# Hash attention and max-out FFN: the projection's split moved to GpSimd, and the last part of w_out loaded earlier, into output tiles

## The chip, the cores and the metric

The kernel runs on one core of one Trainium2 chip. The metric is the device time of a run in microseconds (us), less is better. Engines are called PE (TensorE, matrix multiply), DVE (VectorE), ACT (ScalarE), POOL (GpSimd) and SP (SyncE, which issues most of the DMAs).

## The reference

Attention in which a query sees only the keys that fall in the same hash bucket, followed by a feed-forward layer with a maximum of three products. Batch 4, 8 heads, 768 positions, head size 64, 6 hash bits, model width 512, feed-forward width 768.

```python
q_bits = (einsum('bhsd,dk->bhsk', q, proj) > 0)          # 6 bits of each query
k_bits = (einsum('bhsd,dk->bhsk', k, proj) > 0)
mask   = bucket(q_bits)[..., :, None] == bucket(k_bits)[..., None, :]
scores = where(mask, q @ k.T / sqrt(64), -1e9)
attn   = softmax(scores) @ v                             # (4, 8, 768, 64)
x      = attn.transpose(0, 2, 1, 3).reshape(3072, 512)
h      = maximum(maximum(x @ w1, x @ w2), x @ w3)        # (3072, 768)
out    = h @ w_out                                       # (3072, 512)
```

## The kernel before

The work is cut by batch `b` (0 to 3), pair of heads `pr` (0 to 3) and half of the positions `hf` (0 or 1). For each pair, q, k and v are loaded in float32 (0.39 MB each). q and k are split into two halves in float16 (`split_h`, L266 or L268, and `split_r`, L273), side by side in a tile `s`. That tile is transposed into `T`, in batch 0 and in the first two pairs of batch 1 by PE (L292), later by a DMA transpose on SP's queue (`xbar`, L282). `hash_mm` (L310 and L312) multiplies `T` by `PAB`, the projection in two float16 parts. DVE turns the results into bits, PE transposes these, and they go by way of DRAM (`bit_out`, L349, called the bounce's write, `bit_in`, L352, its read, `T<-dr`) into six rows of `T`. A score matmul (`score`, L395) then gives score and hash agreement at once; ACT takes exponentials (`expo`, L401), and `attend` (L413) multiplies by v. v is cast to float16 by POOL in batch 0 and by ACT (L202) later, where POOL adds it up (`vsum`, L363 to L366) for a small matmul (`svp`, L376). DVE normalizes into `xn`.

For each half of the positions, `xn` becomes `xT` (by PE for the first half, then by a DMA transpose, `x_bar`, L457). `l1` (L478, into `ps`) multiplies by w1, w2 and w3, in 6 blocks of features `fb`, and DVE takes the maximum into `ht` (L487; the first of three is copied, L202 on ACT or L204 on DVE). `l2` (L496, into `po`) multiplies the six `ht` by the six row chunks of `wout_sb`; the result is copied to an output staging tile `osb` (five of them) and stored (L507).

The order of instructions on every engine is fixed when the program is built, by a planner: each task has an engine or two to choose from, an estimated duration, a priority, the tasks it needs, and the counted buffers it takes and gives. The planner runs a small simulation and emits each task at its turn. So the planner's guesses set the order, and the chip keeps to it. Memory on PE's output side is in banks: two for scores (`sc`), one for `av`, three (`mm`) for everything else.

`make_p` makes `PAB` from `p32`, the projection as loaded by ACT's queue at the start: a cast to float16 (`ph`, L234), a difference (`pr32`, L235), and four scalings into `PAB` (L238). It is one task, planned for DVE.

The weights come in parts. w1 and w2 and half of w3 are loaded by POOL's queue with a cast on the way. The second half of w3 (two parts) and w_out (three parts of two row chunks each, 128 x 2 x 512 float32, 0.52 MB) are loaded by SP's queue in float32 into `ws`, of which there are two, by `stage_w`, and cast by POOL into place by `cast_w`:

```python
parts.append(add(("POOL", 1.5 if w == "o" else 1.1), -60, [ld], lambda e, w=w, i=i: cast_w(w, i, e),
                 give=("ws",)))
```

Part 0 has chunks 0 and 1, part 1 has 2 and 3, part 2 has 4 and 5. On SP's queue parts 0 and 1 stand behind the bounce of pair (1,1). Then come q, k and v of pair (2,0), the DMA transpose of pair (1,3), part 2 of w_out, the transpose to `xT` of batch 0's second half, the bounce's write of pair (1,2), and the transpose of pair (2,0). A part takes one of the two `ws`, so part 2 can be loaded only when POOL has cast part 0.

Of the kernel before, what the change touches and what calls it, by code (L numbers as in the profile page):

```python
# [8 lines left out]
FP32 = mybir.dt.float32  # L9
FP16 = mybir.dt.float16  # L10
AluOp = mybir.AluOpType
# [122 lines left out]
def kernel(  # L134
# [12 lines left out]
    nc = tc.nc  # L147
    B, H, S, D = q.shape
    NBITS = proj.shape[1]
    P = 128  # L150
    NCH = S // P
    DM = H * D
# [34 lines left out]
    op = ctx.enter_context(tc.tile_pool(name="op", bufs=OSB))  # L187
# [12 lines left out]
    def copy(e, o, i):  # L200
        if e == "ACT":
            nc.scalar.copy(o, i)  # L202
        else:
            ENG[e].tensor_copy(o, i)  # L204

    p32 = konst.tile([D, NBITS], FP32, name="p32")
# [16 lines left out]
    PAB = konst.tile([P, 2 * NBITS], FP16, name="PAB")  # L223
    xn0 = konst.tile([P, 2, NP, CH, P], FP16, name="xn0")
    w_sb = [konst.tile([P, NJ, DF], FP16, name=f"w{i}_sb") for i in range(3)]
    wout_sb = konst.tile([P, NF, DM], FP16, name="wout_sb")
# [4 lines left out]
    def make_p(e):  # L231
        ph = konst.tile([D, NBITS], FP16, name="ph")
        pr32 = konst.tile([D, NBITS], FP32, name="pr32")
        nc.vector.tensor_copy(ph[:], p32[:])  # L234
        nc.vector.tensor_tensor(out=pr32[:], in0=p32[:], in1=ph[:], op=AluOp.subtract)  # L235
        for o in (0, D):
            for i, src in enumerate((ph, pr32)):
                nc.vector.tensor_scalar(out=PAB[o : o + D, NBITS * i : NBITS * (i + 1)], in0=src[:],  # L238
                                        scalar1=1024.0, scalar2=None, op0=AluOp.mult)


# [1 line left out]
    src = {"q": q, "k": k, "v": v}  # L243
# [279 lines left out]
    def both(dve, act):  # L523
        return [("DVE", dve), ("ACT", act)]

    tp = add("DVE", -200, [], make_p) if False else None
    loads, ready_T, ready_v, ready_m, wload = {}, {}, {}, {}, {}

# [3 lines left out]
    for i, (n, pr, heads) in enumerate(order):  # L532
        half = heads != (0, 2)
        loads[n, 0, pr, heads] = add(("SP", 0.45), -400 + i, [], lambda e, n=n, pr=pr, heads=heads: load(n, 0, pr, heads, e),
                                     take=(n,) if heads[0] == 0 else (), xfer=0.55 if half else 1.1)
    mp = add(("DVE", 0.5), -300, [add(("ACT", 0.1), -500, [], lambda e: None, lat=3.2)], make_p)

    def load_w(i, half, e):
# [111 lines left out]
    wst_tiles = {}  # L650

    def w_view(w, i):
        c = slice(2 * i, 2 * i + 2)
        if w == "o":
            return moe_w_out.rearrange("(c p) m -> p c m", p=P)[:, c, :], wout_sb[:, c, :]
        f = slice(w[0] * DF // 2, (w[0] + 1) * DF // 2)
        return (moe_w1, moe_w2, moe_w3)[w[1]].rearrange("(c p) f -> p c f", p=P)[:, c, f], w_sb[w[1]][:, c, f]

    def stage_w(w, i, e):
        from_dram = w_view(w, i)[0]  # L660
        t = wst.tile([P, 2 * DM], FP32, tag="ws", name="ws")
        wst_tiles[w, i] = t[:, 0 : 2 * from_dram.shape[2]].rearrange("p (c f) -> p c f", c=2)
        nc.sync.dma_start(wst_tiles[w, i], from_dram)  # L663

    def cast_w(w, i, e):
        copy(e, w_view(w, i)[1], wst_tiles.pop((w, i)))

    def weights(b, pr, parts):
        if (pr or b) and parts[0] not in plain and parts[0] != "o":
            prev = add(("POOL", 0.1), -150, [bounced[b, pr]], lambda e: hold(b, pr, e), after=[wprev[0]])  # L670
        elif pr or b:
            prev = bounced[b, pr]
        else:
            prev = ready_v[0, 0]
        for w in parts:
            if w == "o" or w in plain:
                parts = []
                for i in range(NF // 2) if w == "o" else range(NJ // 2):
                    ld = add(("SP", 0.5), -60 if w == "o" else -70, [], lambda e, w=w, i=i: stage_w(w, i, e), take=("ws",),
                             xfer=1.4 if w == "o" else 1.1, after=[prev])  # L680
                    prev = ld
                    parts.append(add(("POOL", 1.5 if w == "o" else 1.1), -60, [ld], lambda e, w=w, i=i: cast_w(w, i, e),
                                     give=("ws",)))
                wload[w] = plan.join(parts, ())
                continue
            else:
                prev = add(("POOL", 0.8), -100, [], lambda e, w=w: load_w(w[1], w[0], e), xfer=2.15, after=[prev])
            wload[w] = prev
        wprev[0] = prev
# [116 lines left out]
```

The softmax here doesn't subtract the row's maximum and nothing guards it: scores larger than these inputs give would overflow.

## Time and profile before

| What | Value |
|---|---|
| Median of 5 runs | 268.95 us (266.16 to 269.76) |
| The profiled execution | 268.95 us, span 267.2 us |
| PE busy | 256.6 us (96% of the span) |
| ACT busy | 196.5 us (74%) |
| DVE busy | 176.4 us (66%) |
| POOL busy | 41.8 us (16%) |
| DMA moved | 41.69 MB, mean 156 GB/s |
| Granted PE clock | 1.000 |
| six operations of `make_p` on DVE | 0.16 to 0.17 us each, from 4.30 us |
| third part of w_out | issued at 70.88 us, POOL casts it from 75.54 us |

The span is the time from the first to the last instruction of the profiled execution; what the run took beyond it lies around the program. Times within the execution are counted from the span's start. In a line of the timeline stand start, duration, engine, line, operation, tiles and, in brackets, how long the engine had been idle and what ended that. A name such as SPq is the engine's queue, in which DMAs are issued. The busy share of an engine is a mean over stages in which different things hold the work up.

### The profile page before, as it was taken

How to read it: one execution, taken by the hardware profiler on the slowest of the kernel's cores; microseconds unless marked ns; L12 is line 12 of the kernel's file. 1: busy time of each engine (PE TensorE's matmuls, PEld its weight loads, DVE VectorE, ACT ScalarE, POOL GpSimd, SP SyncE). 2: the span in 40 equal slices, each digit the busy share in tenths (PEclk: the TensorE clock that was granted, in tenths of full speed). 3: DMA queues.
4: the chain of work that ended last, by engine and by line, in shares of the span. 5: the costliest groups of instructions: out<-in, count | busy, mean ns of one | idle time of the engine just before them, and what ended most of it. 6: DMA issues, size and time to landing. Idle time of an engine off the chain costs nothing.

```text
span 267.2 us, 7323 instructions
## 1 busy us (share of the span) xinstructions
PE 256.6 (96%) x2992; PEld 174.2 (65%) x2992; DVE 176.4 (66%) x394; ACT 196.5 (74%) x283; POOL 41.8 (16%) x57
## 2 busy tenths in 40 slices
PE   7997979999989999999999999999999999999995
PEld 7886757766646666677666767765666656555552
DVE  4998669989855899559885796551655535345260
ACT  5897998987925889999889889898899642332422
POOL 1530054183310333003302030000000000000000
PEclk9999999999999999999999999999999999999999
DMA  6994489699998598995996997212130050120303
GB/s 207 367 264 70 131 261 267 180 262 271 235 240 282 179 230 221 212 256 156 209 229 175 234 179 121 51 32 79 42 61 0 4 163 15 42 79 0 120 0 119
DMA packets 67408, 41.69 MB, mean 156 GB/s; under 512 B 48046, under 2 KB 63662, under 8 KB 67374
## 3 DMA queue, kind: packets, MB, share of 16 engines
q1 hardware_dynamic: 64654, 39.26, 57.1%
q0 software_dynamic: 2640, 1.97, 4.8%
q8 instruction: 23, 0.38, 0.6%
q14 instruction: 11, 0.09, 0.1%
q10 hardware_dynamic: 80, 0.00, 0.0%
HBM read 25.72 MB, written 6.84 MB: 122 GB/s over the span
## 4 chain that ended last, share of the span: by engine, by line
PE 72%; DMA 15%; DVE 5%; SPq 2%; POOL 2%; issue 1%; ACT 0%; ACTq 0%; POOLq 0%
PE ps L478 30%; PE sc L395 17%; PE po L496 11%; PE av L413 9%; DMA dr<-bt 5%; DMA q<-in_q_dram 3%; DMA v<-in_v_dram 3%; PE hps L312 2%; DMA ws<-in_moe_w_dram 2%; DMA ws<-in_moe_w_out_dram 2%; DVE s L273 2%; DVE s L268 1%; SPq L250 1%; SPq L663 1%; DVE T L204 1%
## 5 line engine op out<-in xcount | busy, mean ns | idle before, releaser
L401 ACT ACTIVATE AT<-sc 128x768 f16<-128x768 f32 x192 | 146.3, 814 | 16.2 <-PE sc L395 14.2
L478 PE MATMUL ps<-xT,w_sb 128*128 128x384 f16 x576 | 106.3, 326 | 0.3 <-DVE ht L487 0.3
L395 PE MATMUL sc<-T 128*128 128x384 f16 x384 | 93.0, 325 | 2.2 <-DMA T<-dr 1.4
L487 DVE TENSOR_TENSOR ht<-ht,ps 128x384 f16<-128x384 f16 x96 | 52.9, 551 | 46.4 <-PE ps L478 44.0
L413 PEld LDWEIGHTS <-AT 128*128 128x128 f16 x1152 | 59.5, 97 | 22.8 <-issue 0.2
L478 PEld LDWEIGHTS <-w_sb 128*128 128x128 f16 x576 | 52.7, 98 | 30.8 <-issue 0.9
L413 PE MATMUL av<-vone,AT 128*128 128x65 f16 x1152 | 65.5, 193 | 0.0
L395 PEld LDWEIGHTS <-T 128*128 128x128 f16 x384 | 30.2, 97 | 12.8 <-DMA T<-dr 1.5
L496 PE MATMUL po<-wout_sb,ht 128*128 128x512 f16 (+1 forms) x150 | 33.8, 370 | 0.9 <-POOL wout_sb L204 0.9
L202 ACT CAST ht<-ps 128x384 f16<-128x384 f32 x28 | 13.4, 480 | 26.5 <-DVE ht L487 19.1
L202 ACT COPY osb<-po 128x512 f32<-128x512 f32 (+1 forms) x24 | 13.6, 568 | 18.8 <-PE po L496 18.7
L496 PEld LDWEIGHTS <-ht 128*128 128x128 f16 x150 | 14.1, 98 | 14.8 <-DVE rr L436 1.2
L363 POOL TENSOR_TENSOR vt<-v 128x384 f32<-128x384 f32 x12 | 12.6, 1047 | 67.4 <-DMA v<-in_v_dram 67.4
L430 DVE TENSOR_TENSOR t<-av,mv 128x390 f32<-128x390 f32 x32 | 17.9, 560 | 7.4 <-PE av L413 7.3
L449 DVE TENSOR_TENSOR xn<-t,rr 128x384 f16<-128x384 f32 x32 | 20.5, 641 | 1.1
L273 DVE SCALAR_TENSOR_TENSOR s<-q,s 128x384 f16<-128x384 f32 x32 | 19.2, 615 | 3.0 <-ACT s L266 2.9
L273 DVE SCALAR_TENSOR_TENSOR s<-k,s 128x384 f16<-128x384 f32 x32 | 19.6, 632 | 0.2
L204 DVE CAST ht<-ps 128x384 f16<-128x384 f32 x20 | 11.1, 555 | 10.3 <-PE ps L478 10.1
L292 PE MATMUL tps<-iden,s 128*128 128x128 f16 x168 | 13.4, 220 | 0.8 <-DVE bit L322 0.5
L312 PE MATMUL hps<-PAB,T 128*128 128x12 f16 x336 | 10.7, 168 | 1.4 <-DVE T L204 1.4
L292 PEld LDWEIGHTS <-s 128*128 128x128 f16 x168 | 10.6, 99 | 2.1 <-DVE s L273 1.1
L312 PEld LDWEIGHTS <-T 128*128 128x128 f16 x336 | 10.1, 96 | 2.5 <-DVE T L204 1.5
(54 smaller groups left out, 142.3 us busy)
## 6 DMA issues: line engine op xcount, KB each, us to landing
v<-in_v_dram SPq DMA_DIRECT2D x16, 384.0 KB
out_dram<-osb SPq DMA_DIRECT2D x23, 256.0 KB
q<-in_q_dram SPq DMA_DIRECT2D x15, 384.0 KB
k<-in_k_dram SPq DMA_DIRECT2D x15, 384.0 KB
w_sb<-in_moe_w_dram POOLq DMA_DIRECT2D x5, 384.0 KB, 10.4
ws<-in_moe_w_out_dram SPq DMA_DIRECT2D x3, 512.0 KB
ws<-in_moe_w_dram SPq DMA_DIRECT2D x2, 384.0 KB
dr<-bt SPq DMA_DIRECT2D x15, 36.0 KB
```

Source lines behind the costliest of these rows:

```text
L202: nc.scalar.copy(o, i)
L273: nc.vector.scalar_tensor_tensor(out=s[:, a0:a1, D : 2 * D], in0=raw_view(n, b, pr, heads), scalar=QS, in1=s[:, a0:a1, 0:D], op0=AluOp.mul ...
L292: nc.tensor.transpose(p16[:, c * P : (c + 1) * P], S16[b, pr][:, a0 + c, :], iden[:])
L312: nc.tensor.matmul(o, T[b, pr][:, a, :], PAB[:], start=True, stop=True)
L395: nc.tensor.matmul(sc[:, i, 0:HQ], t[:, NA2 + hh * NCH + 2 * j + i, :], t[:, hh * NCH + hf * CH : hh * NCH + (hf + 1) * CH, :], start=True ...
L401: nc.scalar.activation(AT[:], scs.pop(u)[:, :, 0:HQ], ActFn.Exp, bias=EXP_BIAS, scale=EXP_SCALE)
L413: nc.tensor.matmul(av[:, o : o + D + 1], AT[:, i, c * P : (c + 1) * P], vones[b % 2][:, 2 * pr + hh, 2 * j + i, 0 : D + 1], start=slot == ...
L430: nc.vector.tensor_tensor(out=t[:, :, :, 0 : D + 1], in0=av[:, :, :, 0 : D + 1], in1=mv, op=AluOp.add)
L449: nc.vector.tensor_tensor(out=xv, in0=t[:, :, :, 0:D], in1=rr[:].to_broadcast([P, 2, CH, D]), op=AluOp.mult)
L478: nc.tensor.matmul(ps[:, 0:HQ], w_sb[i][:, jc, fb * P : (fb + 1) * P], xTs[b, hf][:, jc, :], start=jc == 0, stop=jc == NJ - 1)
L487: nc.vector.tensor_tensor(out=ht[:], in0=ht[:], in1=ps[:, 0:HQ], op=AluOp.max)
L496: nc.tensor.matmul(ps[:, m0:m1], hts[b, hf, fb][:, c * P : (c + 1) * P], wout_sb[:, fb, m0:m1], start=fb == 0, stop=fb == NF - 1)
```

## The change

First, all six operations of `make_p` are issued on POOL instead of DVE. The planner still counts them as DVE's.

Second, part 2 of w_out is no longer a load of its own. When part 1 is staged, chunks 4 and 5 are loaded ahead of it as two DMAs of 128 x 512 float32 (0.26 MB each) into two `osb` tiles, and when part 1 is cast, POOL casts these two ahead of it. The tasks of part 2 stay in the plan and emit nothing. So the plan, and with it the order of everything else on every engine, stays as it was. On SP's queue the data of part 2 now stand between parts 0 and 1, ahead of q, k and v of pair (2,0) and the transpose of pair (1,3), and nothing stands between that transpose and the one to `xT`. On POOL all casts of w_out stand ahead of the sums of v of pair (2,0). The planner's counts of `ws` and `osb` do not know of the change.

```diff
     def make_p(e):
...
-        nc.vector.tensor_copy(ph[:], p32[:])
-        nc.vector.tensor_tensor(out=pr32[:], in0=p32[:], in1=ph[:], op=AluOp.subtract)
+        nc.gpsimd.tensor_copy(ph[:], p32[:])
+        nc.gpsimd.tensor_tensor(out=pr32[:], in0=p32[:], in1=ph[:], op=AluOp.subtract)
         for o in (0, D):
             for i, src in enumerate((ph, pr32)):
-                nc.vector.tensor_scalar(out=PAB[o : o + D, NBITS * i : NBITS * (i + 1)], in0=src[:],
+                nc.gpsimd.tensor_scalar(out=PAB[o : o + D, NBITS * i : NBITS * (i + 1)], in0=src[:],
                                         scalar1=1024.0, scalar2=None, op0=AluOp.mult)
...
     def stage_w(w, i, e):
+        if w == "o" and i == 2:
+            return
+        if w == "o" and i == 1:
+            for c in (4, 5):
+                wst_tiles[w, c] = op.tile([P, DM], FP32, tag="osb", name="osb")
+                nc.sync.dma_start(wst_tiles[w, c][:], moe_w_out[c * P : (c + 1) * P, :])
         from_dram = w_view(w, i)[0]
...
     def cast_w(w, i, e):
+        if w == "o" and i == 2:
+            return
+        if w == "o" and i == 1:
+            for c in (4, 5):
+                copy(e, wout_sb[:, c, :], wst_tiles.pop((w, c))[:])
         copy(e, w_view(w, i)[1], wst_tiles.pop((w, i)))
```

## The prediction

> **What bounds the kernel now.** I read the page's first two parts, then the waits of TensorE (PE), then the chain of work that ended last, then the timelines of SP, POOL, ACT and DVE around the one place where the two meet.
>
> ```profile
> PE 256.6 (96%) x2992; PEld 174.2 (65%) x2992; DVE 176.4 (66%) x394; ACT 196.5 (74%) x283; POOL 41.8 (16%) x57
> DMA  6994489699998598995996997212130050120303
> ```
>
> PE is busy 96% of 267.2 us and the clock row is 9 throughout. The order of instructions on each engine is fixed, so the time is PE's work plus the places where PE waits; a PE delay in the middle is not given back, since from 90 to 215 us the table by stretches shows PE busy in all but 0.3 us. DMA is saturated from 53 to 80 us (its row, slices of 6.7 us). In the waits of PE between 60 and 90 us one line counts:
>
> ```profile
> PE po L496 <- POOL wout_sb L204: 0.9, 1, 0.9
> ```
>
> The chain of waits between 60 and 86 us (start, duration, what) says how this wait comes about:
>
> ```profile
> 62.99 7.06 DMA v<-in_v_dram
> 70.13 0.75 POOL vt L363
> 70.88 4.61 DMA ws<-in_moe_w_out_dram
> 75.54 1.05 POOL wout_sb L204
> 76.62 0.59 PE po L496 x2
> ```
>
> The third part of w_out is issued at 70.88, lands at about 75.5, is cast by POOL until 76.6, and only then the last two of six matmuls of the first output group run. Why it is issued so late is in SP's queue (start, time in the queue, line, what):
>
> ```profile
> 59.60 2.32 SPq L663 DMA_DIRECT2D ws<-in_moe_w_out_dram  x2
> 61.97 0.47 SPq L250 DMA_DIRECT2D q<-in_q_dram  x1
> 62.49 0.46 SPq L250 DMA_DIRECT2D k<-in_k_dram  x1
> 62.99 0.47 SPq L250 DMA_DIRECT2D v<-in_v_dram  x1
> 63.56 7.21 SPq L282 DMA_TRANSPOSE T<-s  x1
> 70.88 0.52 SPq L663 DMA_DIRECT2D ws<-in_moe_w_out_dram  x1
> 71.49 2.46 SPq L457 DMA_TRANSPOSE xT<-xn  x1
> ```
>
> It stands behind the transpose of pair (1,3), which is itself held up by the 1.15 MB of q, k and v of pair (2,0) ahead of it.
>
> **Edit 1, six small operations from DVE to POOL.** DVE loses six operations of about 0.16 us; from 4.30 to 5.14 us that is 0.84 us of its queue, and the split of k behind them starts up to 0.75 us sooner. What it gains is swallowed here:
>
> ```profile
> 7.95 0.56 DVE L273 SCALAR_TENSOR_TENSOR s<-q,s 128x384 f16<-128x384 f32 x1 [0.39 <-ACT s L266]
> L647 POOL COPY hold<-T x1: 183/183/183, 35.8 to 35.8; 6x1 f16<-6x1 f16 x1
> ```
>
> The chain at the start is q's load (until 7.05), ACT's split (7.07, 0.84 us), then this DVE operation at 7.95. Neither end of it moves; DVE's idle before it grows from 0.39 to about 1.1 us. The hash bits (L322, 8.43) are queued behind it on DVE, so nothing later moves either. Gain 0; without that load as cover it would be worth up to 0.75.
>
> On POOL the six wait for the load of proj. It had landed by 4.30 (DVE ran its cast there without waiting). The nearest POOL row is the copy of 6x1 above, 0.183 us: 6 x 0.18 = 1.1, done by 5.4. The dear end is the 128x128 add of L365, 0.64 us: 6 x 0.64 = 3.8, done by 8.1. The hash matmuls (L310, 7.03 to 7.77) need the result, and the bits read them at 8.43, so they may slip 0.66 us, to 7.69. The edit costs between 0 and 8.1 - 7.69 = 0.4; I take 0. The next POOL work is the cast of v at 9.51, later than both.
>
> **Edit 2, what it takes away.** The third part no longer needs one of the two ws tiles nor the place behind the transpose. The four po matmuls issued from 74.68 take 0.216 us each (six take 1.30 in the chain), so the fifth would have been issued at 75.54; it came at 76.62. At most 1.08 us of PE go (0.9 of pure waiting, the rest is refilling the pipe). What PE would meet next is the hash matmul of pair (1,3), whose transpose was in before the w_out part that landed at 75.5, and then L478 at 80.36, needing xT; neither waited.
>
> **Edit 2, what it moves.** Now 0.52 MB more stands ahead of q, k and v of pair (2,0), as two DMAs of 0.26 MB. This is what I think decides. The cost per part is read from when POOL's casts could start:
>
> ```profile
> 63.80 1.04 POOL L204 CAST wout_sb<-ws 128x1024 f16<-128x1024 f32 x1 [4.39 <-DMA ws<-in_moe_w_out_dram]
> 65.17 1.04 POOL L204 CAST wout_sb<-ws 128x1024 f16<-128x1024 f32 x1 [0.33 <-DMA ws<-in_moe_w_out_dram]
> ```
>
> Two parts of 0.52 MB landed 1.37 us apart. That is the cheap end. The dear end: from 65.17 to v's landing at about 70.1, 1.18 MB took 4.9 us, so 0.52 MB at that rate takes 2.2. A rule of the Trainium skill speaks against the edit more strongly: "DMA: Bandwidth & Descriptors", section "Anatomy of one DMA — SWDGE (gpsimd) path", gives a DMA 2.0 us fixed plus its bytes at 436 GB/s (fitted for DMAs issued by GpSimd). By it two of 0.26 MB are 2 x 2.6 = 5.2 us if they follow one another, and the sum would be +4.1. The row shows 1.37 us for twice the bytes of one of them, so queued loads hide the fixed part. I go by the row, with a little for the second DMA: 1.5 us later for q, k and v.
>
> Who waits for these three:
>
> ```profile
> 68.98 0.56 DVE L268 TENSOR_SCALAR s<-k 128x768 f16<-128x768 f32 x1 [0.43 <-DMA k<-in_k_dram]
> 68.55 1.51 ACT L401 ACTIVATE AT<-sc 128x768 f16<-128x768 f32 x2
> 70.13 0.83 ACT L202 CAST vone<-v 128x768 f16<-128x768 f32 x1
> 70.87 1.50 ACT L401 ACTIVATE AT<-sc 128x768 f16<-128x768 f32 x2
> ```
>
> ACT came to the cast of v at 70.06 and began at 70.13, as v landed: no slack at all. Behind it on ACT are the exponentials of the last four score tiles of this stretch and one ht evacuation. With two sc banks, the score matmuls at 71.94 and 72.45 wait for the exponentials ahead of them, and the attend matmuls up to 74.50 for the rest; PE has nothing else in its order. So PE reaches po about 1.5 us later, at 76.2. DVE already waited 0.43 for k, and will wait some 1.5 more in all, with two ht evacuations (69.93, 71.49) behind it; with three mm banks that stays inside PE's 1.5 us. POOL's sums of v end at about 74.3, before the svp matmul (73.80 + 1.5).
>
> **Edit 2, the rest.** SP issues one DMA more ahead of q (about 0.45 us); the data ahead arrive later than that, so it is hidden. Three POOL casts (0.5, 0.5, 1.04 us, halves of the row) stand ahead of POOL's sums of v, done by about 68, before v is in. Two of the five osb tiles are in use until then; the first output copy is at 77.25. The transpose of (1,3) ends 1.5 us later, but the w_out load behind it is gone: xT, the bounce of (1,2) and the next transpose have the same bytes ahead as before. One change from plain loads to a transpose and back goes too, and around such a change the DMA rate is low (68 GB/s from 69 to 70 us against 263 to 367 from 64 to 67). So I expect nothing late after 77 us.
>
> **Sum.** PE +1.5 (v late) - 1.08 (w_out no longer late) = +0.4; edit 1 adds 0. The profiled execution took 268.95 us (span 267.2 and 1.75 around it), and the median of the five runs is the same 268.95: **269.4 us**. The runs spread from 266.16 to 269.76, so about 1% (2.7 us) is what a measurement of this kernel can tell from no change.
>
> **Rivals.**
> *The load is nearly hidden (0.26).* For it: DMA is not full when w_out starts (115 GB/s from 60 to 61, 199 from 62 to 63), and k's late landing may not recur. If v comes only 0 to 0.7 us later, PE gains 0.4 to 1.08: 267.9 to 268.6. Against it: the queue is served in order and ACT has no slack.
> *The bounce of pair (1,2) comes too late (0.15).* It is the read T<-dr that SP issued at 79.28, behind the transpose of (2,0), which waits for DVE's split of k. The score matmul at 84.91 needs it and ACT stands empty before that. The read took 2.4 us alone (chain, 23.93); 79.28 + 2.4 = 81.7 leaves at most 3.2 us, less in the crowd. If the transfers ahead slip by over 3 us (the rule's 5.2 for the added loads would do it), PE has lost 2 by v already (3 - 1.08) and waits another 0.5 to 2.5 here: 271.5 to 273.5, slower. For it: the queue is full. Against it: the bytes ahead are unchanged.
> *POOL's projection is slow (0.05).* If an operation costs L363's 1.05 us, PAB is ready at 10.6, 2.9 us after 7.69; with +0.4 that is 272.2. The 6x1 copy speaks against it.
> That the third part is not early at all is excluded by SP's order.
>
> **How the numbers follow.** The main case has 0.54 (v 1.4 to 2.2 us late, 269.2 to 270.1). Nearly hidden 0.26, late bounce 0.15, slow POOL 0.05. The range takes in the bounds of v's delay, the hidden case and the spread of the runs: 267.0 to 271.7. Over 1% slower are the late bounce and part of slow POOL, 0.17; over 1% faster needs more than the 1.08 us that PE can gain, so only an unseen gain or spread, 0.08; the rest, 0.75, is within 1%.
>
> **What would show it.** After: no wait of po on wout_sb; ACT idle 1.4 to 2.2 us before the cast of v at about 71.6, put down to the DMA of v; DVE idle longer before L268 of q and k; PE idle in 70 to 76 in place of 76; the first output copy at 77.5 to 78 instead of 77.25; DVE idle about 1.1 us before 7.95. Wrong if v lands as before, if PE waits for T<-dr near 85, or if the first hash matmul waits for POOL.

## The result, and the profile after

The changed kernel's median is 269.63 us over 43 runs (266.76 to 272.62), beside 268.23 us over 80 runs of the kernel before on the same chips (265.68 to 272.04). The ratio is **1.0035, with a 95% interval of 1.0017 to 1.0053**: 0.9 us more (0.5 to 1.4; 0.0035 x 268.23). The ratio leaves out slow runs, among them seven of the changed kernel at 270.8 to 272.6 us, which the medians contain. The forecast was 269.4 us, with 267.0 to 271.7 as its range and "within 1%" as its likeliest case. So the total came out as forecast. Its terms did not: what the forecast adds up around 70 us comes to about nothing, and the place where every profile with the added DMA shows a loss is the end of the program, which it left out. That is what the rest is about. Microseconds for a ratio are always worked out on 268.2 us.

The profiled execution of the changed kernel took 268.62 us (span 266.8), less than its median and less than the 268.95 of before. One profile of each can't show a difference of 0.9 us; it can show where waits went. First, the rows of PE and DMA on the page of the changed kernel:

```profile
PE 256.8 (96%) x2992; PEld 175.1 (66%) x2992; DVE 174.5 (65%) x388; ACT 196.8 (74%) x283; POOL 44.6 (17%) x64
DMA  6994599699998897998992995302030060110303
```

PE's work is unchanged. DVE has lost six instructions, POOL has gained seven (six of `make_p`, and two casts of half a part for one of a whole). SP's queue in the changed kernel (start, time in the queue, line, what) is as the diff says:

```profile
59.27 0.92 SPq L665 DMA_DIRECT2D osb<-in_moe_w_out_dram  x2
60.29 1.62 SPq L669 DMA_DIRECT2D ws<-in_moe_w_out_dram  x1
61.95 0.48 SPq L250 DMA_DIRECT2D q<-in_q_dram  x1
62.48 0.47 SPq L250 DMA_DIRECT2D k<-in_k_dram  x1
62.99 0.47 SPq L250 DMA_DIRECT2D v<-in_v_dram  x1
63.56 7.38 SPq L282 DMA_TRANSPOSE T<-s  x1
71.05 1.44 SPq L457 DMA_TRANSPOSE xT<-xn  x1
```

q, k and v are issued at 61.97 to 62.99 in the one and 61.95 to 62.99 in the other, and the transpose to `xT` starts 0.44 us earlier. The first output group now runs without a break, and PE waits in another place before it (timeline of PE, changed kernel):

```profile
70.32 0.34 PE L413 MATMUL av<-vone,AT 128*128 128x65 f16 x6 [0.27 <-DVE t L430]
74.79 1.46 PE L496 MATMUL po<-wout_sb,ht 128*128 128x512 f16 x6
```

The wait of 0.9 for `wout_sb` is gone; one of 0.27 for DVE has come. The first output copy starts at 76.28 instead of 77.25. What holds that DVE operation up is in the chain of waits of the changed kernel between 60 and 86 us:

```profile
61.95 5.66 DMA q<-in_q_dram
67.61 0.02 issue
67.64 0.04 DVE s L268
67.67 0.44 issue
68.11 0.28 DVE bt L344
68.39 0.82 DVE s L273 x2
69.21 0.03 issue
69.25 0.55 DVE s L268
69.80 0.48 DVE t L430
70.28 0.04 issue
70.32 0.34 PE av L413 x6
```

Read it from below: the attend matmul needs the one `av` bank, which L430 frees; on DVE L430 stands behind the splits of k and q of pair (2,0), and these stand behind the load of q. ACT's cast of v, which the forecast had on the path, starts at about the same time, and this matmul does not wait for it (timelines of ACT and DVE, changed kernel):

```profile
70.27 0.83 ACT L202 CAST vone<-v 128x768 f16<-128x768 f32 x1 [0.91 <-DMA v<-in_v_dram]
67.64 0.56 DVE L268 TENSOR_SCALAR s<-q 128x768 f16<-128x768 f32 x1 [1.51 <-DMA q<-in_q_dram]
```

ACT took v at 70.27, against 70.13 before: not 1.5 us later. The table by stretches (length; busy time of PE, PEld, DVE, ACT and POOL; clock, DMA share, GB/s) tells why. The kernel before, from 60 us:

```profile
60.00:62.00 2.00, 2.00 (x28) 1.41 (x25) 2.00 (x5) 1.60 (x3) 0.00 (x0) 1.00 0.72 206
62.00:64.00 2.00, 2.00 (x19) 1.26 (x18) 1.86 (x7) 2.00 (x5) 0.20 (x1) 1.00 0.89 262
```

The same of the changed kernel:

```profile
60.00:62.00 2.00, 2.00 (x24) 1.36 (x23) 2.00 (x5) 1.65 (x3) 0.00 (x0) 1.00 0.91 265
62.00:64.00 2.00, 2.00 (x19) 1.26 (x17) 1.86 (x6) 2.00 (x4) 0.00 (x0) 1.00 1.05 373
```

In these 4 us the changed kernel moved 0.34 MB more ((265 + 373 - 206 - 262) GB/s x 2 us). Most of the added 0.52 MB went through at times when the DMA engines had been short of work.

At the start of the program, POOL's six operations (changed kernel):

```profile
3.47 0.18 POOL L234 CAST ph<-p 64x6 f16<-64x6 f32 x1 [2.16 <-DMA p<-in_proj_dram]
4.02 0.46 POOL L238 TENSOR_SCALAR PAB<-ph 64x6 f16<-64x6 f16 x1
5.30 0.23 POOL L238 TENSOR_SCALAR PAB<-pr 64x6 f16<-64x6 f32 x1
```

They end at 5.53, well ahead of the first hash matmul at 7.28. And DVE, where the forecast looked at 7.95:

```profile
5.57 0.56 DVE L204 COPY T<-tps 128x768 f16<-128x768 f16 x1 [0.73 <-PE tps L292]
8.21 0.56 DVE L273 SCALAR_TENSOR_TENSOR s<-q,s 128x384 f16<-128x384 f32 x1 [0.44 <-ACT s L266]
```

DVE lost its 0.7 us right at 5.57 already, to a wait for PE's transposes, and the operation of 7.95 starts at 8.21, as its load came later in this execution.

At the end of the program, PE's last matmuls in the kernel before (timeline of PE) and what SP waits for from 262 us on (us in total, times, longest; L801 closes the program):

```profile
259.90 4.06 PE L496 MATMUL po<-wout_sb,ht 128*128 128x512 f16 x24
SPq L801 <- DMA out_dram<-osb: 0.7, 2, 0.5
```

The same of the changed kernel:

```profile
258.83 4.06 PE L496 MATMUL po<-wout_sb,ht 128*128 128x512 f16 x24
SPq L812 <- DMA out_dram<-osb: 1.7, 1, 1.7
```

PE ends at 263.96 in the one and at 262.89 in the other, 1.07 us earlier, but the spans end at 267.17 and 266.85, only 0.32 us apart. So 0.75 us more pass behind PE. The reason is in the records of SP. A semaphore tells of a DMA's landing; ACT's load of proj and SP's DMAs take eight of them in turn, and at the end SP waits for the eight in a fixed order. Before, the last store is SP's 127th DMA and its semaphore the eighth in that order, so that the other seven waits are over when it lands. With part 2 as two DMAs it is the 128th and its semaphore the first, and the other seven waits come behind it, 0.06 us each. Counted from the start of the last matmul, the last store is issued at 0.75 before and at 0.91 after, lands at 2.56 and 2.91, and SP's eight waits are over at 2.60 and 3.37.

### The profile page after: what moved, and what is told of

It reads as the page before. It is cut to its first block, busy times and chain, and to the rows that moved or that the text cites. A ratio compares the mean times of both kernels' runs of the same rounds, so it can differ in the third digit from the quotient of the medians.

```text
span 266.8 us, 7327 instructions
## 1 busy us (share of the span) xinstructions
PE 256.8 (96%) x2992; PEld 175.1 (66%) x2992; DVE 174.5 (65%) x388; ACT 196.8 (74%) x283; POOL 44.6 (17%) x64
## 4 chain that ended last, share of the span: by engine, by line
PE 78%; DMA 8%; DVE 6%; SPq 3%; ACT 3%; issue 1%; POOL 1%; ACTq 0%; POOLq 0%
PE ps L478 31%; PE sc L395 19%; PE po L496 11%; PE av L413 10%; DMA q<-in_q_dram 4%; DMA v<-in_v_dram 3%; PE hps L312 2%; ACT AT L401 2%; DVE s L273 2%; PE tps L292 2%; SPq L669 1%; DVE s L268 1%; SPq L250 1%; DMA T<-dr 1%; DVE xn L449 1%
## 5 line engine op out<-in xcount | busy, mean ns | idle before, releaser
L430 DVE TENSOR_TENSOR t<-av,mv 128x390 f32<-128x390 f32 x32 | 17.9, 560 | 8.2 <-PE av L413 8.1
L449 DVE TENSOR_TENSOR xn<-t,rr 128x384 f16<-128x384 f32 x32 | 19.6, 611 | 1.1
L273 DVE SCALAR_TENSOR_TENSOR s<-k,s 128x384 f16<-128x384 f32 x32 | 18.7, 605 | 0.1
L202 ACT CAST vone<-v 128x768 f16<-128x768 f32 x12 | 10.0, 834 | 1.7 <-DMA v<-in_v_dram 1.7
```

What stands on the lines that cost most here:

```text
L273: nc.vector.scalar_tensor_tensor(out=s[:, a0:a1, D : 2 * D], in0=raw_view(n, b, pr, heads), scalar=QS, in1=s[:, a0:a1, 0:D], op0=AluOp.mul ...
L430: nc.vector.tensor_tensor(out=t[:, :, :, 0 : D + 1], in0=av[:, :, :, 0 : D + 1], in1=mv, op=AluOp.add)
L449: nc.vector.tensor_tensor(out=xv, in0=t[:, :, :, 0:D], in1=rr[:].to_broadcast([P, 2, CH, D]), op=AluOp.mult)
```

## The experiments

The accounts that are told apart: the forecast's (the bytes ahead of v reach PE through ACT); its rival that DVE's splits of q and k carry the delay to PE; that the delay hardly exists; and that the gain at `po` is smaller than in the profile, or given back later. The end of the program was in none of them; no run was made for it, and it is read from the profiles of all. Beside the ratios I use one more measure. The order of the matmuls is the same in all kernels here. For each matmul, the time from the start of the one before it to its own start is taken in 14 profiled executions, and the shortest is subtracted. What is left is PE's loss at that place, us. The column "end" is the time from the start of the last matmul to the end of the span:

| Kernel | third part at `po` | `av` behind L430 (70.6) | `sc` behind ACT (71.9) | `bps` (104.25) | end | ratio, 95% interval |
|---|---|---|---|---|---|---|
| before | 1.08 | 0 | 0 | 0 | 3.48 | |
| before again (e8) | 0.19 | 0 | 0 | 0.31 | 3.40 | 1.0012, 0.9984 to 1.0040 |
| edit 1 alone (e1) | 0.38 | 0 | 0 | 0.32 | 3.36 | 1.0024, 0.9993 to 1.0056 |
| edit 1 alone again (e11) | 0.50 | 0 | 0 | 0.57 | 3.39 | 0.9970, 0.9939 to 1.0001 |
| third part left out (e4) | 0 | 0 | 0 | 0.84 | 3.44 | 0.9996, 0.9970 to 1.0023 |
| third part behind v (e3) | 0 | 0 | 0 | 0.83 | 4.24 | 1.0031, 1.0001 to 1.0061 |
| e3 with late sums (e6) | 0 | 0 | 0 | 0 | 4.31 | 1.0021, 0.9995 to 1.0047 |
| edit 2 alone (e2) | 0 | 0.17 | 0 | 0.55 | 4.27 | 1.0057, 1.0031 to 1.0083 |
| the change | 0 | 0.43 | 0.21 | 0.58 | 4.23 | 1.0035, 1.0017 to 1.0053 |
| the change again (e7) | 0 | 0 | 0 | 0.60 | 4.22 | 1.0027, 1.0000 to 1.0053 |
| edit 2 and 0.52 MB more (e5) | 0 | 2.66 | 0.14 | 0.58 | 4.13 | 1.0096, 1.0060 to 1.0133 |
| e5 with v first (e9) | 0 | 3.32 | 0.16 | 0.85 | 4.15 | 1.0156, 1.0097 to 1.0215 |
| e5 with q and k early (e10) | 0 | 0 | 2.49 | 0.32 | 4.18 | 1.0145, 1.0085 to 1.0205 |
| the change, q and k early (e12) | 0 | 0 | 0.79 | 0.57 | 4.55 | 1.0000, 0.9969 to 1.0031 |

The times in the head are those of the kernel before. In e6, PE lost 0.35 at the small matmul `svp` that follows 2 us later.

The end is 3.36 to 3.48 us in the five kernels in which SP issues 127 DMAs (e4: 126), and 4.13 to 4.55 in the nine in which it issues 128 or, in e5, e9 and e10, 130. Against the means of the four executions of the old order (0.54 at `po`, 0.30 at `bps`, 3.41 at the end), the places of this table and the end add up to 0.0 us for e4 (measured -0.1), +0.8 for e3 (+0.8), +0.4 for e6 (+0.6), +0.6 for e7 (+0.7), +1.2 for the change (+0.9), +3.3 for e5 (+2.6), +4.2 for e9 (+4.2) and +2.7 for e10 (+3.9). For e2 (+0.7, measured +1.5) and e12 (+1.7, measured 0.0) the sum lies outside the interval.

### Each edit alone, and the part behind v

**e1_projection_on_pool** is the kernel before with edit 1 only:

```diff
-        nc.vector.tensor_copy(ph[:], p32[:])
+        nc.gpsimd.tensor_copy(ph[:], p32[:])
...
```

> Edit 1 alone: the projection's six operations on POOL, w_out loaded as before. Theory A (v's delay decides): nothing moves behind the q load at the start, PAB is ready on POOL by about 5.5 us and the first hash matmul needs it at 7.0, so ratio 1.000 (268.2 us in the median of before). Rival B (edit 1 is the loss): the whole +0.9 us of the change is here, ratio 1.0035, and the first score matmul starts about 0.9 us later against the landing of q.

Measured: 1.0024 (0.9993 to 1.0056), +0.6 us with an interval that holds zero. I ran the same kernel once more, as **e11_projection_again**:

> Edit 1 alone again (1.0024, interval 0.9993 to 1.0056 the first time), to say whether it has a share. Theory A: 1.000. Rival B: 1.0024 or more.

Measured: 0.9970 (0.9939 to 1.0001), -0.8 us. The two lie on both sides of 1 and their mean is 0.9997. Edit 1 makes no difference that shows here, and two results of one kernel can be half a per cent apart.

**e2_wout_ahead_of_q** is the kernel before with edit 2 only (the second and third hunk of the diff).

> Edit 2 alone: chunks 4 and 5 of w_out loaded into two osb tiles ahead of part 1 and so ahead of q, k and v of pair (2,0); the projection stays on DVE. Theory A: all of the change's loss is here: v 1.4 to 2.2 us later, 1.08 us won at po, ratio 1.001 to 1.004. Rival B: ratio 1.000 or below. Rival C (the wait moved is paid back, and the loss comes later, at the bounces): ratio as in A, but ACT's wait for v is under 1 us and a score matmul after 84 us waits for T<-dr.

Measured: 1.0057 (1.0031 to 1.0083), +1.5 us (0.8 to 2.2). What the change costs, edit 2 costs. The ratio lies above the range that was expected, though in its profile ACT waited only 0.24 us for v.

**e3_wout_behind_v** loads the two chunks behind v of pair (2,0) and ahead of the transpose of (1,3), and casts them at part 2's old place on POOL:

```diff
     def xbar(b, pr, e):
+        if (b, pr) == (1, 3):
+            for c in (4, 5):
+                wst_tiles["o", c] = op.tile([P, DM], FP32, tag="osb", name="osb")
+                nc.sync.dma_start(wst_tiles["o", c][:], moe_w_out[c * P : (c + 1) * P, :])
...
     def cast_w(w, i, e):
         if w == "o" and i == 2:
+            for c in (4, 5):
+                copy(e, wout_sb[:, c, :], wst_tiles.pop((w, c))[:])
             return
```

> Chunks 4 and 5 go into two osb tiles as in the change, but are issued behind v of pair (2,0) and ahead of the transpose of pair (1,3), and POOL casts them behind its sums of v; the projection stays on DVE. Theory A: v lands as before, the two chunks land by about 72 us and are cast by 74.5, before po needs them at 75.5, so PE keeps the 1.08 us: ratio 0.996 (267.1 us). Rival C (the transposes and bounces behind are what counts): they have 0.5 MB more ahead than before, so ratio 1.000 to 1.004.

Measured: 1.0031 (1.0001 to 1.0061), +0.8 us. The part is in time (no loss at `po`), v is not delayed (4.5 us from POOL's cast of part 0 to its first sum of v, against 4.9 to 6.3 in the four executions of the old order), and still there is no gain: PE lost 0.83 at 104 us, of which more below, and the end is 4.24.

**e4_wout_part_left_out** does not load the third part:

```diff
     def stage_w(w, i, e):
+        if w == "o" and i == 2:
+            return
...
+        if w == "o" and i == 1:
+            copy(e, wout_sb[:, 4:6, :], wst_tiles[w, i])
         copy(e, w_view(w, i)[1], wst_tiles.pop((w, i)))
```

> The third part of w_out is not loaded at all; POOL casts part 1 twice, so rows 512 to 767 of w_out are replaced by a copy of rows 256 to 511. This is the ceiling of what an early third part can bring. Theory A: 1.08 us at po, and 0.5 MB less for the transposes behind, ratio 0.996 to 0.994. If the wait at po were covered by something else that comes as late (xT or the bounce), ratio 1.000.

Measured: 0.9996 (0.9970 to 1.0023), -0.1 us (-0.8 to +0.6). This is the ceiling for edit 2: the part never late, nothing in its place, and an end as before (3.44). It is worth nothing that shows, and a gain of 1.08 us, as in the first profile, lies outside the interval.

### Why the ceiling is so low

**e8_before_again** is the kernel before, unchanged.

> The kernel before again, as a control: ratio 1.000 with its interval, and a second profile that shows how much the wait of po for w_out (0.9 us in the first) and the waits between 20 and 60 us vary from execution to execution. Theory A needs a wait of po of 0.4 to 1 us here; if it is 0, the first profile overstated the gain.

Measured: 1.0012 (0.9984 to 1.0040). In its profile PE does not wait for `wout_sb` by name at all, and loses 0.19. The old order has four profiled executions (before, e8, e1, e11): 1.08, 0.19, 0.38 and 0.50, mean 0.54. The first profile showed the worst of the four.

The rest goes at 104 us, at the hash bits of pair (2,1). In DVE's order the splits of q of pair (2,3) stand ahead of these bits, and at that time POOL adds up v of pair (2,3). Two engines meet there. DVE and POOL in the kernel before:

```profile
101.63 1.02 DVE L273 SCALAR_TENSOR_TENSOR s<-q,s 128x384 f16<-128x384 f32 x2
103.96 1.38 DVE L273 SCALAR_TENSOR_TENSOR s<-k,s 128x384 f16<-128x384 f32 x1
103.90 1.02 POOL L363 TENSOR_TENSOR vt<-v 128x384 f32<-128x384 f32 x1 [6.70 <-DMA v<-in_v_dram]
```

DVE, POOL and PE in the changed kernel:

```profile
100.86 1.85 DVE L273 SCALAR_TENSOR_TENSOR s<-q,s 128x384 f16<-128x384 f32 x2
100.93 1.37 POOL L363 TENSOR_TENSOR vt<-v 128x384 f32<-128x384 f32 x1 [5.22 <-DMA v<-in_v_dram]
104.06 0.30 PE L339 MATMUL bps<-iden,bit 128*72 128x128 f16 x2 [0.41 <-DVE bit L332]
```

And in e4:

```profile
100.13 2.11 DVE L273 SCALAR_TENSOR_TENSOR s<-q,s 128x384 f16<-128x384 f32 x2
103.58 0.30 PE L339 MATMUL bps<-iden,bit 128*72 128x128 f16 x2 [0.68 <-DVE bit L332]
```

Before, POOL's sum of v fell on the second part of k, which no matmul was waiting for, and stretched that one to 1.38. With v in earlier, it falls on the second part of q, which DVE has to finish before the bits; the pair takes 1.85 or 2.11 instead of 1.02, and PE waits for the bits. The old order can meet this too: in e11 the pair took 1.84 us, and PE lost 0.57.

**e6_behind_v_late_sums** tests this. It is e3, in which POOL makes a copy of one column of the bits of pair (2,1) ahead of the sums of v of (2,3), so that these start later:

```diff
     def vsum(b, pr, e):
...
+        if (b, pr) == (2, 3):
+            late = small.tile([P, 1], FP16, tag="late", name="late")
+            nc.gpsimd.tensor_copy(late[:], kept_bits[2, 1][:, 0, 0, 0:1])
```

> As the variant with the two chunks behind v, and one tiny POOL copy of a hash bit of pair (2,1) ahead of POOL's sums of v of pair (2,3), so that these start only after the bits at about 103 us. Theory E (what is won at po is lost near 104 us, where POOL's first sum now falls on DVE's split residual of q, L273, which then takes 1.8 to 2.1 us for two instead of 1.0, and PE waits 0.5 to 0.8 us for the bits): DVE's two take about 1.0 us, PE's wait for the bits is gone, ratio 0.2 to 0.3% below the variant without it: 1.000 to 1.001. Rival (the DMA rate or the DVE order holds the bits): DVE's two still take about 2 us, and the ratio stays at 1.003.

DVE and POOL in e6:

```profile
100.45 1.02 DVE L274 SCALAR_TENSOR_TENSOR s<-q,s 128x384 f16<-128x384 f32 x2
102.92 0.45 POOL L369 COPY late<-bit 128x1 f16<-128x1 f16 x1 [7.63 <-DVE bit L337]
```

The pair is back at 1.02 and PE's loss at the bits at 0, from 0.83 in e3. So the collision is shown, and so is that it costs these 0.8 us at that place. The sums are now so late that `svp` loses 0.35. Measured: 1.0021 (0.9995 to 1.0047); against e3's 1.0031 that is no difference that can be told.

### What carries the delay to PE

The delay of the change itself is small, so I doubled it. **e5_more_ahead_of_q** is edit 2 with two more loads of 0.26 MB that nobody reads:

```diff
         if w == "o" and i == 1:
...
+            for c in (0, 1):
+                t = op.tile([P, DM], FP32, tag="osb", name="osb")
+                nc.sync.dma_start(t[:], moe_w_out[c * P : (c + 1) * P, :])
```

> As edit 2 alone, with two more loads of 0.26 MB (chunks 0 and 1 of w_out again, into two osb tiles that nobody reads) ahead of q, k and v of pair (2,0). Theory A (what stands ahead of v is paid by PE, since ACT's cast of v has no slack): v lands another 1.4 to 2.2 us later and PE loses that much more: ratio 1.009 to 1.014, with ACT idle 2.5 to 4 us before the cast of v. Rival D (the transfers' order is not what costs, the rest of the program makes up for it): ratio as with edit 2 alone, 1.003 to 1.008.

Measured: 1.0096 (1.0060 to 1.0133), +2.6 us, 1.0 more than e2 (0.39% of 268.2; the two intervals overlap). The time from POOL's cast of part 0 to its first sum of v is 8.4 us, against 6.2 to 6.5 with 0.52 MB ahead (the change, e7, e2; mean 6.3) and 4.9 to 6.3 with nothing (mean 5.8). By these means the first 0.52 MB cost v about 0.5 us and the next 2.1. The 0.5 is less than the spread of the old order; with e3, e4 and e6 (4.5, 5.4 and 4.5 us), in which the same loads stand ahead of v as in the old order, it would be 0.9. PE's waits between 60 and 90 us in e5 (engine, line, waited for: us in total, times, longest):

```profile
PE av L413 <- DVE t L430: 2.5, 1, 2.5
```

DVE is named, not ACT; but q and v are late together in e5. Two kernels take one of them away. **e9_more_ahead_v_first** is e5 with v ahead of q and k:

```diff
+    def load(n, b, pr, heads, e):
+        if (b, pr) == (2, 0):
+            for m in {"q": "vq", "k": "k", "v": ""}[n]:
+                load1(m, b, pr, heads, e)
...
```

> As the variant with two more loads ahead of q, k and v of pair (2,0) (1.0096; PE's one wait there 2.66 us, at the attend matmul behind DVE's L430), but with v loaded ahead of q and k. Theory A as predicted (ACT's cast of v carries the delay to PE): v lands about 2.4 us sooner, PE's stall between 70 and 76 us shrinks to under 1 us, ratio 1.002 to 1.006. Theory F (DVE carries it: the splits of q and k wait in front of L430, which frees the one av bank): k lands about 1.2 us later still, the stall grows to 3.5 to 4 us, ratio 1.010 to 1.015.

Measured, in four runs: 1.0156 (1.0097 to 1.0215). ACT takes v without waiting, and PE waits for DVE all the same. PE's waits between 60 and 90 us in e9:

```profile
PE av L420 <- DVE t L437: 3.2, 1, 3.2
```

And DVE's timeline in e9, where q now stands behind v:

```profile
69.63 0.56 DVE L275 TENSOR_SCALAR s<-q 128x768 f16<-128x768 f32 x1 [4.08 <-DMA q<-in_q_dram]
```

**e10_more_ahead_qk_early** is e5 with q and k issued right behind part 0, ahead of all the added loads, and v behind them:

```diff
         if w == "o" and i == 1:
+            load1("q", 2, 0, (0, 2), "SP")
+            load1("k", 2, 0, (0, 2), "SP")
             for c in (4, 5):
...
```

> As the variant with two more loads, but q and k of pair (2,0) are issued right behind part 0 of w_out, ahead of the other five loads; v stays behind all of them. Theory A (ACT's cast of v): v lands as late as without this, ACT is idle 2.5 to 3 us before it, PE still stalls 2.5 to 3 us, ratio 1.008 to 1.012. Theory F (DVE): no wait of DVE for q or k, L430 is on time; PE's stall is what ACT alone can do: if F is the whole of it, under 0.5 us, ratio 1.000 to 1.004.

Measured, in four runs: 1.0145 (1.0085 to 1.0205). Now DVE is in time, and PE waits for ACT, which waits for v. PE's waits between 60 and 90 us in e10:

```profile
PE sc L399 <- ACT AT L405: 2.3, 1, 2.3
```

And ACT's timeline in e10:

```profile
73.44 0.83 ACT L202 CAST vone<-v 128x768 f16<-128x768 f32 x1 [2.78 <-DMA v<-in_v_dram]
```

So both ways to PE exist, side by side. With v freed, DVE costs 3.3 us; with q and k freed, ACT costs 2.5. When all three are late, as in e5, DVE's is felt first and ACT's is mostly hidden behind it.

**e12_change_qk_early** moves q and k ahead in the same way in the changed kernel itself.

> The change (both edits) with q and k of pair (2,0) issued right behind part 0 of w_out, so that DVE's splits do not wait; v is as late as in the change. Theory F: PE does not stall before po, and the ratio falls to the level of the variant without the third part, 0.998 to 1.001. Theory A: no better than the change, 1.002 to 1.006.

Measured: 1.0000 (0.9969 to 1.0031). The loss behind DVE is gone, and 0.79 has come behind ACT. The ratio is the best of the kernels with edit 2, but its interval overlaps that of the change, and it does not beat the kernel before. Its losses in the table and its end (4.55) do not show in the ratio. On the same chip e11, with the old order, stood at 0.9970; that may be a part of it, and the rest is open.

**e7_change_again** is the changed kernel once more, beside the others on their chip.

> The changed kernel again, for a second profile and a tighter ratio. Theory A: ratio 1.002 to 1.006; ACT idle 0.7 to 2 us before the cast of v at 70 us, no wait of po for w_out.

Measured: 1.0027 (1.0000 to 1.0053), in agreement with the result. In its profile the added delay costs PE nothing at `av`, and ACT does not wait for v.

## Why the prediction was right, and where its steps were not

- **"Edit 1 ... I take 0": right**, by e1 and e11 together. Two sizes in it were off. "6 x 0.18" gave 5.4; the cast and the difference took 0.18 and 0.19, but the four scalings 0.23 to 0.46, and the end was 5.53, with two microseconds to spare. And the cover is another than I named: what DVE saves goes into a wait of 0.73 us for PE's transposes at 5.57, not into one of 1.1 before 7.95.
- **"At most 1.08 us of PE go": right as a bound, twice the size of what goes.** Four executions of the old order show 0.54 in the mean. I read a wait's size from a single execution and put it in the sum as if it were always that.
- **"I go by the row, with a little for the second DMA: 1.5 us later": about twice to three times too much.** The first 0.52 MB cost 0.5 to 0.9 us. The row of 1.37 us is one execution's, taken with the queue full (in e8, with the same order, the two casts start 3.13 us apart); the added loads went out at 59 to 60 us, where 206 and 262 GB/s left room (slices of 6.7 us had hidden that in the row that I called saturated). I had that as a rival's argument ("DMA is not full when w_out starts") and gave it no weight in the sum. The second 0.52 MB cost 2.1 us, close to the dear end of 2.2. Did each queued DMA pay a fixed 2.0 us in its turn, the four that e5 adds would take 4 x 2.6 = 10.4 us (an estimate from the Trainium skill's "DMA: Bandwidth & Descriptors", section "Anatomy of one DMA — SWDGE (gpsimd) path", which gives the rule for one DMA); v was 2.6 us later (8.4 - 5.8).
- **"ACT has no slack", DVE "stays inside PE's 1.5 us": half wrong.** I counted what stands behind L268 on DVE as two `ht` evacuations and missed L430, which frees the only `av` bank. In the change and in e5 that was the first to hold PE. ACT is a second way of nearly equal length, as e10 shows.
- **"I expect nothing late after 77 us": wrong.** At the hash bits, the loss is 0.58 in the change, and 0.30 in the mean of the four executions of the old order (0, 0.31, 0.32, 0.57). That gives back 0.28. And the end of the program, which the forecast does not look at, is 0.83 us longer (mean of 4.23, 4.22 and 4.27, against 3.41).
- **The sum: the right total by luck.** I had +1.5 - 1.08 = +0.4. By the losses of the profiled executions with edit 2 in the change's form (the change, e7, e2) it is +0.2 at `av` (mean of 0.43, 0 and 0.17), +0.07 at `sc`, +0.28 at the bits, -0.54 at `po`: nothing. The first term was 1.2 too large, the second 0.5, and the bits bring 0.3. The end, +0.83, is alone close to the measured +0.9 (0.5 to 1.4), and the forecast had nothing there. Its base helped too: 268.95 is 0.7 us above the median of 80 runs.
- **Its own signs.** "Wrong if v lands as before" is nearly what the profile shows (70.27 against 70.13), ACT waited 0.91 us for v and not 1.4 to 2.2, and the first output copy came at 76.28 and not at 77.5 to 78. By these signs the delay that the forecast counted on was not there, though `po` does not wait for `wout_sb` any more.
- **Left open.** The end differs by 0.8 us between all profiles with the added DMA and all without, and the order of SP's waits accounts for 0.4 of it; why the last store is issued 0.16 us later and takes 2.0 us to land and not 1.8 is not shown. The kernel before with one more small DMA on SP's queue would test it alone. Nor do the profiles give the whole of the +0.9: over all matmuls from 60 us on, the three executions lost 0.5 us less than the four of the old order, in part at places that vary, so that their spans are only 0.3 us longer in the mean (266.2 against 265.9). e2 and e12 do not fit, as said above. With the kernel before against itself at 1.0012, a few tenths of a microsecond cannot be placed.
- **The rivals.** "Nearly hidden" was the right picture of the load, with the wrong total, since the gain was smaller too and the end longer. The late bounce did not come: PE's waits from 60 to 110 us in the changed kernel name no `T<-dr`. Slow POOL did not come either.

## What to carry to other kernels

Take the size of a wait from several executions before it goes into a sum: here the same wait on the same kernel was worth 0.2 to 1.1 us, and taking it away altogether was worth nothing that could be measured. Where a load is put ahead of others, price it by the room that the queue has in those very microseconds, and follow each delayed load through the whole order of its engine up to the operation that frees a bank for PE. And when data come earlier, look for the engine that starts earlier with them, and at what that will collide. Last, compare the time behind the last matmul: one DMA more can move the end of the program.

## What was unexpected of the hardware

- An addition on POOL (128x384, both inputs in SBUF) and DVE's two residuals of q (also with both inputs in SBUF) do not run side by side at full speed: DVE's pair took 1.85 and 2.11 us instead of 1.02, POOL's 1.37 instead of 1.02. The Trainium skill's "SBUF — State Buffer", section "Who interferes with whom", says that a DVE instruction with two SBUF inputs contends with a GpSimd instruction that reads SBUF, through a shared pair of ports under an exclusive lock. Did the three never overlap, they would need about 1.02 + 1.02 = 2.04 us (an estimate from the rows and that rule). From the first start to the last end they took 2.49 us in e4 but 1.85 in the change, so there they overlap in part; that it is this port is the page's explanation, and no run here separates it from another.
- Splitting one load on SP's queue into two moved the last store to another of eight semaphores, and the program ended 0.8 us later behind its last matmul: 4.13 to 4.55 us in nine executions with the added DMA, against 3.36 to 3.48 in five without.
- The same small scaling took 0.16 to 0.17 us on DVE and 0.23 to 0.46 on POOL.
- The start of the program differs between executions of one kernel: DVE's operation of 7.95 us in the kernel before started at 9.20 in e8, and the execution was still the shorter one (span 264.6 against 267.2 us).
